# One activation table set in a fused DiT block, with layer-norm roots taken in pairs

## The chip, the cores and the metric

The kernel runs on one core of one Trainium2 chip. The metric is device time in microseconds (us); lower is better. Nearly every execution also leaves its span (first to last instruction, about 1.8 us shorter than the time) and its mean granted TensorE clock, where 1.0 is full speed. Ratios below are the mean time of one kernel's fast runs over that of the other's of the same rounds, so they are not quite the ratio of the medians quoted beside them.

## The reference, cut to what matters

```python
B, N, D = 2, 256, 1152          # F = 4 * D, two heads, bf16 inputs
mod = (silu(c) @ w_mod)         # shift_a, scale_a, gate_a, shift_m, scale_m, gate_m
h   = layernorm(x) * (1 + scale_a) + shift_a          # LN1
q, k, v = split(h @ wqkv)
a   = softmax(q k^T / sqrt(Dh)) @ v @ wo
x   = x + gate_a * a
h2  = layernorm(x) * (1 + scale_m) + shift_m          # LN2
out = x + gate_m * (gelu(h2 @ w_fc1) @ w_fc2)
```

## The kernel before

The 512 tokens are four tiles `t` of 128 rows: tiles 0 and 1 are batch 0, tiles 2 and 3 batch 1. While x and the first weights arrive, TensorE (PE) runs warm-up matmuls on zeros. LN1's statistics are split: VectorE (DVE) takes tiles 1 and 3, ScalarE (ACT) tiles 0 and 2. Each inverse root is a `pow` on GpSimd (Pool), one column at a time. Each normalized tile is transposed on PE, multiplied by 1 + scale ("modulate"), and fed to the K projection step by step. The order below is the program order on every engine.

```python
warm(8, pwarm)                    # fp32 matmuls on zeros
act_stats(0); act_stats(2)        # ACT: sums and sums of squares
...                               # DVE: bn_stats of tile 1
rsqrt1(1, True)                   # Pool: add eps, pow
act_mean(0)                       # Pool mean; DVE dm2; Pool dm2 += eps
act_var(0)                        # DVE
rsqrt1(0, False)                  # Pool: pow
norm1(1, 0, CUT)
stats_piece(3, 0)
norm1(0, 0, CUT)
stats_piece(3, 1); stats_piece(3, 2)
rsqrt1(3, True)
act_mean(2)
pt_a = transpose_x([0, 1], BT[0])         # PE, batch 0
add0 = scale_group(0, 1, acc_tile)        # 9 matmuls: scale chunk 0
add1 = scale_group(1, 2, acc_tile)        # 9 matmuls: scale chunk 1
add0()                                    # DVE: + 1
modulate(pt_a, 0, 0, 0, 0, "a")
act_var(2)
rsqrt1(2, False)
add1()
modulate(pt_a, 1, 1, 0, 0, "a")
norm1(3, 0, CUT); norm1(2, 0, CUT)
k_step(0, 0, N); k_step(1, 0, N, 0, 3)    # PE: K, batch 0
pt_c = transpose_x([0, 1], BT[1])         # PE, batch 1
...
# LN2, per tile: ACT Sqrt(var + eps), DVE reciprocal
```

## Time and profile before

| | before |
|---|---|
| median of the three first runs | 246.46 us (246.21 to 247.16) |
| the profiled execution | 245.73 us, span 244.0 us, clock 1.0 |
| PE busy | 237.0 us, 97% of the span |
| PE from 13.2 us on | 17.61 busy of 17.83 us up to 31 us, and no gap over 0.05 us in the chain after that |

From the profile's page: the span, PE's busy time, and the granted clock in 40 slices of 6.1 us (9 means 90% or more).

```profile
span 244.0 us, 3979 instructions
PE 237.0 (97%) x1688; PEld 145.0 (59%) x1698; DVE 91.2 (37%) x194; ACT 61.7 (25%) x117; POOL 30.1 (12%) x49
...
PEclk9999999999999999999999999999999999999999
```

PE is the limit almost everywhere, so time can only be won where PE waits: in the ramp at the start. The next view is the timeline of PE in that ramp (columns: start, duration, engine, line, operation, output and inputs, shape, count, and in brackets the idle time before it and what ended it).

```profile
9.20 0.38 PE L240 MATMUL pt<-ident,xn 128*128 128x128 bf16 x4 [0.40 <-ACT xn L191]
9.71 0.60 PE L230 MATMUL pm<-sT,w_scale_a 128*128 128x2 bf16 x18
10.89 0.71 PE L256 MATMUL pk<-big,w_k 128*128 128x256 bf16 x5 [0.57 <-ACT big L248]
11.97 0.27 PE L256 MATMUL pk<-big,w_k 128*128 128x256 bf16 x1 [0.37 <-DVE scale_a L234]
...
13.17 0.40 PE L240 MATMUL pt<-ident,xn 128*128 128x128 bf16 x4 [0.20 <-DVE xn L218]
```

L240 are the transposes (`pt`: first batch 0, then at 13.17 batch 1), L230 the modulation matmuls for the first two scale chunks, L256 the K projection. Why batch 1's transposes wait until 13.17 is told by the chain of waits (start, duration, what):

```profile
10.64 0.57 POOL rstd L215
11.21 0.26 POOL mv L198
11.47 0.19 POOL dm L204
...
11.93 0.74 POOL rstd L215
...
13.17 0.41 PE pt L240 x4
```

Two Pool powers (L215, 0.57 and 0.74 us), with a mean (L198) and an addition of eps (L204) on Pool and a variance on DVE between them, stand one after the other between batch 1's statistics and its transposes.

The ScalarE timeline has four table loads:

```profile
1.39 1.28 ACT L153 ACT_TABLE_LOAD   x1 [1.39 <-PEq L783]
54.54 1.28 ACT L524 ACT_TABLE_LOAD   x1
80.06 1.28 ACT L611 ACT_TABLE_LOAD   x1
107.20 1.28 ACT L697 ACT_TABLE_LOAD   x1 [1.36 <-issue]
```

Those at 54.54 and 80.06 us, ahead of softmax and LN2, are the two that the change removes.

### The profile page before, as it was taken

The page shows a single profiled execution, that of the slowest core. Times are in us where ns is not written, and L with a number is a line of the kernel's source. Part 1 is how long each engine was busy: PE and PEld are TensorE (multiplying, and loading weights), DVE is VectorE, ACT ScalarE, POOL GpSimd, SP SyncE. Part 2 cuts the span into 40 slices and gives each one's busy share as a digit, 9 for nine tenths or more (in the row PEclk, how much of TensorE's full clock was granted, in tenths as well). Part 3 has the DMA queues.
Part 4 walks back from the last instruction along what each step waited for, and adds up shares of the span by engine and source line. Part 5 has one row for each costly group of instructions (what it writes and reads, how often), then busy time and mean ns, then how long its engine had stood idle before and what let it go on. Part 6 is the DMA issues. An engine that isn't in the chain of part 4 may idle for free.

```text
span 244.0 us, 3979 instructions
## 1 busy us (share of the span) xinstructions
PE 237.0 (97%) x1688; PEld 145.0 (59%) x1698; DVE 91.2 (37%) x194; ACT 61.7 (25%) x117; POOL 30.1 (12%) x49
## 2 busy tenths in 40 slices
PE   8799999999999999999999999999999999999994
PEld 5575444456667556788854444444566666656574
DVE  3552542325515588932001999960010000000001
ACT  6623332235323321563432222332000000000000
POOL 2500000031000232300000000001112221111111
PEclk9999999999999999999999999999999999999999
DMA  6999999994779998248999999199630000000000
GB/s 209 323 317 319 380 370 390 391 392 167 172 235 396 391 377 133 47 81 294 394 388 392 350 327 318 33 336 326 194 108 16 20 16 16 20 16 16 24 28 16
DMA packets 48781, 53.29 MB, mean 218 GB/s; under 512 B 9587, under 2 KB 36475, under 8 KB 48763
## 3 DMA queue, kind: packets, MB, share of 16 engines
q1 hardware_dynamic: 41312, 50.14, 61.6%
q10 hardware_dynamic: 6939, 1.71, 4.6%
q0 software_dynamic: 512, 1.19, 1.6%
q8 instruction: 13, 0.21, 0.4%
q14 instruction: 5, 0.04, 0.1%
HBM read 50.14 MB, written 1.19 MB: 210 GB/s over the span
## 4 chain that ended last, share of the span: by engine, by line
PE 93%; DVE 2%; DMA 1%; POOL 1%; issue 1%; SPq 0%; POOLq 0%; DVEq 0%
PE pacc L744 29%; PE pacc L688 29%; PE pacc L634 7%; PE pacc L544 7%; PE pq L465 7%; PE pk L256 4%; PE pk L285 2%; PE pa L582 2%; PE ps_s L502 2%; PE pn L363 2%; DMA x_sb<-in_x_dram 1%; DVE stats L180 1%; PE pt L240 1%; POOL rstd L215 1%; PE pm L230 1%
## 5 line engine op out<-in xcount | busy, mean ns | idle before, releaser
L688 PE MATMUL pacc<-hT,w_f 128*128 128x256 bf16 (+1 forms) x427 | 70.3, 325 | 0.3
L744 PE MATMUL pacc<-w_f,gT 128*128 128x384 bf16 (+2 forms) x468 | 70.5, 314 | 0.0
L744 PEld LDWEIGHTS <-gT 128*128 128x128 bf16 x468 | 44.4, 98 | 26.2
L688 PEld LDWEIGHTS <-w_f 128*128 128x128 bf16 x432 | 42.2, 98 | 27.6
L750 DVE TENSOR_TENSOR tmp<-pacc,gate 128x384 f32<-128x384 f32 (+2 forms) x13 | 6.9, 527 | 65.6 <-PE pacc L744 55.0
L720 ACT ACTIVATE gT<-pacc 128x512 bf16<-128x512 f32 x24 | 14.3, 597 | 32.6 <-PE pacc L688 32.6
L416 DVE SCALAR_TENSOR_TENSOR part<-w_gate_m,s,part 128x1152 f32<-128x1152 bf16 x16 | 21.4, 1413 | 0.0
L634 PE MATMUL pacc<-w_o,big 128*128 128x384 bf16 x108 | 18.1, 326 | 0.0
L752 POOL TENSOR_TENSOR o_sb<-tmp,x 128x384 bf16<-128x384 f32 (+1 forms) x12 | 11.7, 972 | 51.8 <-DVE tmp L750 51.8
L465 PE MATMUL pq<-hT,w_q 128*128 128x512 bf16 x79 | 17.9, 379 | 0.1
L544 PE MATMUL pacc<-w_v,hT 128*128 128x384 bf16 x108 | 17.7, 326 | 0.0
L256 PE MATMUL pk<-big,w_k 128*128 128x256 bf16 (+1 forms) x70 | 13.4, 324 | 1.4 <-ACT big L248 0.8
L544 PEld LDWEIGHTS <-hT 128*128 128x128 bf16 x108 | 10.5, 98 | 7.1 <-issue 0.2
L634 PEld LDWEIGHTS <-big 128*128 128x128 bf16 x108 | 10.3, 98 | 7.3 <-issue 0.7
L465 PEld LDWEIGHTS <-w_q 128*128 128x128 bf16 x81 | 7.8, 98 | 9.4 <-issue 0.3
L640 POOL TENSOR_TENSOR x<-tmp,x_sb 128x384 f32<-128x384 f32 x8 | 7.3, 914 | 33.5 <-DVE tmp L639 33.5
L414 DVE TENSOR_SCALAR part<-w_gate_m,s 128x1152 f32<-128x1152 bf16 x2 | 1.5, 818 | 22.0 <-DMA w_gate_m<-in_w_mod_dram 22.0
L256 PEld LDWEIGHTS <-w_k 128*128 128x128 bf16 x72 | 6.7, 97 | 5.2 <-issue 1.8
L438 POOL DMA_DIRECT2D gates_dram<-nat_v x2 | 1.1, 536 | 67.5 <-DVE nat_v L436 67.5
L709 ACT ACTIVATE gT<-pacc 128x512 bf16<-128x512 f32 x12 | 6.5, 598 | 9.0 <-PE pacc L688 9.0
L162 PE MATMUL pwarm<-zeros 128*128 128x256 f32 x20 | 7.6, 549 | 1.2 <-DVE eps_t L93 1.2
L639 DVE TENSOR_TENSOR tmp<-pacc,gate 128x384 f32<-128x384 f32 x12 | 6.6, 551 | 3.7 <-PE pacc L634 3.7
(92 smaller groups left out, 163.2 us busy)
## 6 DMA issues: line engine op xcount, KB each, us to landing
w_f<-in_w_fc_dram SPq DMA_DIRECT2D x12, 864.0 KB, 14.8
w_f<-in_w_fc_dram SPq DMA_DIRECT2D x3, 1728.0 KB, 8.1
w_f<-in_w_fc_dram SPq DMA_DIRECT2D x2, 2592.0 KB, 18.2
w_gate_a<-in_w_mod_dram SPq DMA_DIRECT2D x3, 864.0 KB, 12.3
w_v<-in_wqkv_dram SPq DMA_DIRECT2D x3, 864.0 KB, 14.1
w_o<-in_wo_dram SPq DMA_DIRECT2D x3, 864.0 KB, 14.3
w_shift_m<-in_w_mod_dram SPq DMA_DIRECT2D x3, 864.0 KB, 6.5
w_scale_m<-in_w_mod_dram SPq DMA_DIRECT2D x3, 864.0 KB, 12.1
```

Of the source, the lines that this page charges most:

```text
L162: nc.tensor.matmul(dst[:, 0:T // 2], zeros32[:, 0:P], zeros32, start=True, stop=True)
L256: nc.tensor.matmul(pk[m][:, c0:c1], w_k[:, k, m * P:(m + 1) * P], hT0[:, k, c0:c1], start=(k == 0 and c0 == 0), stop=(k == KD - 1), skip_g ...
L416: nc.vector.scalar_tensor_tensor(part[:, b, :], wg[:, k, :], s32[:, k, b:b + 1], part[:, b, :], op0=ALU.mult, op1=ALU.add,)
L465: nc.tensor.matmul(pq[m][:], w_q[:, k, m * P:(m + 1) * P], hT[:, k, :], start=(k == 0), stop=(k == KD - 1), skip_group_check=True,)
L544: nc.tensor.matmul(pacc[:], hT[:, k, t * P:(t + 1) * P], w_v[:, k, pnl * PW:(pnl + 1) * PW], start=(k == 0), stop=(k == KD - 1),)
L634: nc.tensor.matmul(pacc[:], aT[:, k, t * P:(t + 1) * P], w_o[:, k, c0:c1], start=(k == 0), stop=(k == KD - 1),)
L640: (nc.gpsimd if pool_add else nc.vector).tensor_tensor(x1[:, t, c0:c1], tmp[:], x_sb[:, t, c0:c1], op=ALU.add)
L688: nc.tensor.matmul(dst, w_f1[m // KD][:, k, ml * P:(ml + 1) * P], hT[:, k, c0:c1], start=start, stop=(k == KD - 1), **kw,)
L720: nc.scalar.activation(gT[:, m, :], pacc[:], ACT.Gelu_apprx_tanh)
L744: nc.tensor.matmul(pacc[:], gT[:, kk, t * P:(t + 1) * P], w_f2[j][:, r, c0 - n * PW:c0 - n * PW + cw], start=(kk == 0), stop=(kk == KF - 1),)
L750: nc.vector.tensor_tensor(tmp[:], pacc[:], gate_m[:, b, c0:c0 + cw], op=ALU.mult)
L752: (nc.vector if last else nc.gpsimd).tensor_tensor(o_sb[:], tmp[:], x1[:, t, c0:c0 + cw], op=ALU.add)
```

## The change

The intent: Silu becomes c / (1 + exp(-c)), and LN2's inverse root becomes exp(-ln(var + eps) / 2), so Exp and Ln from one table set serve everything up to the Gelu. In LN1, batch 0's two roots become one two-column Pool pow, and batch 1's two roots an Ln and an Exp on ScalarE. The first two scale chunks share one PSUM tile (the buffer that the matmuls write to) and one addition, on ScalarE. The first modulate moves from ScalarE ("a") to VectorE ("d"), and the transposes go tile by tile, which the cut leaves out. Cut to its core:

```diff
-    nc.scalar.activation(early[:, 0:1], zeros[:, 0:1], ACT.Silu)
+    nc.scalar.add_instruction(mybir.InstLoadActFuncSet(act_func_set_id=6, ...))   # ln and exp
...
-    nc.scalar.activation(sT..., pc..., ACT.Silu)
+    nc.scalar.activation(sig[:], pc[:], ACT.Exp, scale=-1.0)
+    nc.vector.tensor_scalar_add(sig[:], sig[:], 1.0)
+    nc.vector.reciprocal(sig[:], sig[:])
+    nc.vector.tensor_tensor(sT..., pc..., sig..., op=ALU.mult)
...
+    def ln_exp_rsqrt(dst, var):
+        nc.scalar.activation(dst, var, ACT.Ln, bias=eps_t[:], scale=1.0)
+        nc.scalar.activation(dst, dst, ACT.Exp, scale=-0.5)
...                                           # the ramp
-    rsqrt1(1, True)
-    act_mean(0)
+    act_mean(0, True)
+    nc.gpsimd.tensor_scalar_add(mv1[:, 1, 1:2], mv1[:, 1, 1:2], LN_EPS)
     act_var(0)
-    rsqrt1(0, False)
-    norm1(1, 0, CUT)
+    var, rstd = pair(0)
+    nc.gpsimd.tensor_tensor(rstd, var, neg_half[:], op=ALU.pow)
     stats_piece(3, 0)
     norm1(0, 0, CUT)
+    norm1(1, 0, CUT)
     stats_piece(3, 1)
+    act_mean(2, False)
     stats_piece(3, 2)
-    rsqrt1(3, True)
-    act_mean(2)
+    act_var(2)
     pt_a = transpose_x([0, 1], BT[0])
-    add0 = scale_group(0, 1, acc_tile)
-    add1 = scale_group(1, 2, acc_tile)
-    add0()
-    modulate(pt_a, 0, 0, 0, 0, "a")
-    act_var(2)
-    rsqrt1(2, False)
-    add1()
+    add = scale_group(0, 2)
+    add()                                     # on ScalarE: Identity, bias 1
+    modulate(pt_a, 0, 0, 0, 0, "d")
+    var, rstd = pair(2)
+    ln_exp_rsqrt(rstd, var)
     modulate(pt_a, 1, 1, 0, 0, "a")
+    norm1(2, 0, CUT)
     norm1(3, 0, CUT)
-    norm1(2, 0, CUT)
...                                           # LN2
-        nc.scalar.activation(rstd[:], mv2[:, t, 1:2], ACT.Sqrt, bias=eps_t[:], scale=1.0)
+        ln_exp_rsqrt(rstd[:], mv2[:, t, 1:2])
-        nc.vector.reciprocal(rstd[:], rstd[:])
```

## The prediction

> What bounds the kernel now. TensorE: the page gives PE 237.0 of 244.0 us busy at full granted clock, and the chain of waits is 93% PE. From 13.17 us to the last output PE hardly waits (windows: 17.61 busy of 17.83 us up to 31 us, full after that). Before 9.20 us PE only runs warm-up matmuls. So time can be won only in the ramp from 9.2 to 13.2 us: there PE has 32 matmuls, some 1.9 us of work at the later pace, in 3.97 us. The waits list and the timeline name the stalls: 0.57 us before the first K matmul (behind the scale's add and ScalarE's 0.47 us modulate), 0.37 us on the second scale add's PSUM buffer, 0.24 us on the second modulate, and 0.2 us at 13.17 behind batch 1's norm. There the chain goes VectorE variance, Pool 0.22, 0.57, 0.27, 0.19 us, VectorE, Pool pow 0.73 us (to 12.67), norm, transposes.

> Removed. Two of four table loads, 1.28 us each in the timeline (at 54.5 us before softmax, 80.1 us before the Sqrt). Both are hidden: after the softmax load ScalarE still waits 2.64 us for VectorE, after the Sqrt load 6.93 us. Worth nothing. [...]

> Added. Silu's three VectorE instructions of 0.15 to 0.2 us run at 3.7 to 4.4 us, where VectorE idles until x lands at 4.46. Free.

> Moved. Batch 0: one Pool pow over two columns, my estimate 0.6 to 0.95 us, from 7.1 us. Normalizes start near 8.1 instead of 8.64 (now batch 0's second) and end near 8.9, transposes at 8.8 to 9.2. But the first scale weights land at 9.66 (PE weight load waited 0.30 us for them), so 18 modulation matmuls again run 9.71 to 10.31: this part wins nothing. Then ScalarE's add of one (0.28 us) and VectorE's 0.35 us modulate: first K matmul at about 11.05, 0.15 us later than now. ScalarE then does Ln and Exp (about 0.3 us each, to 11.2) and the second modulate (to 11.65), just in time for PE. Norms of batch 1 run 11.25 to 12.0 instead of 11.8 to 13.1, so its transposes start at about 12.1 to 12.2 instead of 13.17. From there PE is full as before: 1.0 us gained, and kept. Thin point: the third group of scale weights lands at about 15.9 and would be wanted at 16.3.

> LN2: Ln, Exp on ScalarE replace Sqrt and VectorE's reciprocal: rstd about 0.05 to 0.1 us later per tile (0.35 us for tile 2's modulates). PE has no wait there; the first FC1 matmul at 99.77 has about 0.35 us of slack. Zero.

> Predicted: 245.4 us, 244.5 to 246.4. Faster by over 2%: 0.01; within 2%: 0.98; slower by over 2%: 0.01.

> Signs that it's right: first batch 1 transpose near 12.1 us; first K matmul near 11.05; PE idle between 9.2 and 14 us down by 1 us; two table loads; the FC1 start and every later mark about 1 us earlier; no PE wait near 99 us.

> Wrong if: the two-column pow takes well over 1.4 us; the third variance comes late on VectorE and Ln waits; scale weights arrive late so PE stalls at 16 us; LN2's longer root delays the first FC1 matmul; a table load stays somewhere in the ramp.

The sum: 246.46 us less the ramp's 1.0 to 1.1 us (batch 1's transposes at 12.1 to 12.2 instead of 13.17) is 245.4 us; the table loads, the added VectorE instructions and LN2 count zero. The times of instructions that the kernel before doesn't have are estimates; its profile shows 0.57 to 0.73 us for a one-column pow on Pool, 0.29 us for a 128x1 Sqrt on ScalarE, 0.35 us for a VectorE modulate and 0.15 us for its addition of one.

## The result, and the profile after

The changed kernel takes 244.22 us (median of 4 runs, 244.12 to 244.6), before 246.49 us (4 runs), ratio 0.9907 (95% interval 0.9884 to 0.993). 2.3 us were gained where 1.06 was forecast, and 244.22 lies below the stated range. The gain between the two profiled spans is 1.6 us (244.0 to 242.4).

The page after:

```profile
span 242.4 us, 3980 instructions
PE 236.4 (98%) x1688; PEld 145.2 (60%) x1698; DVE 91.2 (38%) x192; ACT 59.8 (25%) x120; POOL 27.8 (11%) x45
...
PEclk9999999999999999999999999999999999999999
```

The table loads on ScalarE after. Two are left, as intended; LN1's Ln at 10.14 us and Exp at 10.46 us, softmax's exponentials and LN2's roots all run between them without a third:

```profile
1.39 1.28 ACT L153 ACT_TABLE_LOAD   x1 [1.39 <-PEq L799]
105.65 1.28 ACT L713 ACT_TABLE_LOAD   x1 [1.36 <-issue]
```

The timeline of PE in the ramp after (L258 transposes, L244 modulation, L274 K):

```profile
8.66 0.39 PE L258 MATMUL pt<-ident,xn 128*128 128x128 bf16 x4
9.28 0.60 PE L244 MATMUL pm<-sT,w_scale_a 128*128 128x2 bf16 x18 [0.23 <-DMA w_scale_a<-in_w_mod_dram]
10.68 1.14 PE L274 MATMUL pk<-big,w_k 128*128 128x256 bf16 x9 [0.80 <-DVE big L264]
11.66 0.39 PE L258 MATMUL pt<-ident,xn 128*128 128x128 bf16 x4
11.89 1.42 PE L274 MATMUL pk<-big,w_k 128*128 128x256 bf16 x9
```

The first K matmul starts at 10.68 instead of 10.89 us, batch 1's transposes at 11.66 instead of 13.17 us. After that PE is full again in both, and what follows is the same: from the first K matmul of batch 1 that waits for its modulate (14.01 and 12.49 us) to the first FC1 matmul it is 85.76 us in both (99.77 and 98.25), and from there to PE's end 141.03 us in both. The 1.52 us are won in the ramp and kept to the end. One sign of the prediction was missed: PE's idle time between 9.2 and 14 us fell from 1.63 to 0.99 us, by 0.64 us and not by 1 us. Part of the gain lies earlier, where the first transposes start at 8.66 instead of 9.20 us.

The chain of waits in the ramp after:

```profile
2.58 6.65 DMA w_scale_a<-in_w_mod_dram
...
9.28 0.62 PE pm L244 x18
...
9.98 0.27 ACT scale_a L250
...
10.68 1.14 PE pk L274 x9
```

Pool and the norms have left the chain. It now starts from the arrival of the first scale weights (`w_scale_a`), which landed at 9.23 us here; in the profile of before they landed at about 9.66 us.

That leaves two questions. The prediction had batch 1's transposes at 12.1 to 12.2 us: is the missing 0.45 us only the earlier landing, and is that luck or the change? And why is the gain by medians, 2.27 us, larger than the 1.6 us between the spans?

### The profile page after: what moved, and what is told of

Same layout as the page of the kernel before. It is cut to its first block, busy times and chain, and to the rows that moved or that the text cites. A ratio compares the mean times of both kernels' runs of the same rounds, so it can differ in the third digit from the quotient of the medians.

```text
span 242.4 us, 3980 instructions
## 1 busy us (share of the span) xinstructions
PE 236.4 (98%) x1688; PEld 145.2 (60%) x1698; DVE 91.2 (38%) x192; ACT 59.8 (25%) x120; POOL 27.8 (11%) x45
## 4 chain that ended last, share of the span: by engine, by line
PE 94%; DMA 3%; SPq 1%; DVE 1%; issue 0%; ACT 0%; DVEq 0%; ACTq 0%
PE pacc L760 29%; PE pacc L704 29%; PE pacc L650 7%; PE pacc L561 7%; PE pq L482 7%; PE pk L274 5%; DMA w_scale_a<-in_w_mod_dram 3%; PE pk L303 2%; PE pa L599 2%; PE ps_s L519 2%; PE pn L380 2%; PE pm L244 1%; PE pt L258 1%; SPq L86 1%; PE pg L462 0%
## 5 line engine op out<-in xcount | busy, mean ns | idle before, releaser
L768 POOL TENSOR_TENSOR o_sb<-tmp,x 128x384 bf16<-128x384 f32 (+1 forms) x12 | 11.6, 970 | 54.2 <-DVE tmp L766 54.2
L274 PE MATMUL pk<-big,w_k 128*128 128x256 bf16 (+1 forms) x70 | 13.1, 324 | 1.0 <-DVE big L264 0.8
L274 PEld LDWEIGHTS <-w_k 128*128 128x128 bf16 x72 | 6.7, 98 | 4.5 <-issue 1.1
```

Source lines behind the costliest of these rows:

```text
L274: nc.tensor.matmul(pk[m][:, c0:c1], w_k[:, k, m * P:(m + 1) * P], hT0[:, k, c0:c1], start=(k == 0 and c0 == 0), stop=(k == KD - 1), skip_g ...
L768: (nc.vector if last else nc.gpsimd).tensor_tensor(o_sb[:], tmp[:], x1[:, t, c0:c0 + cw], op=ALU.add)
```

## The experiments

Four runs went to each chip together, and each kernel was executed five or six times there, beside 11 executions of the kernel before. Every execution comes with a mean clock, and this is what turned out to matter. (It reads 1.0 also where nothing was recorded: the profiles of e4 and e9 hold no clock record. Their matmuls in the ramp took the times of the other full-clock profiles, 1.14 and 1.42 us for two groups of nine K matmuls, so these two were at full clock; for the other executions it can't be checked.) The table sums up all of them; "full clock" means a mean clock of 0.998 or more, "low clock" 0.993 or less; nothing lay between.

| kernel | executions | at full clock: mean time, mean span | at low clock: number, mean time |
|---|---|---|---|
| before (e1 and the three sets beside the experiments) | 39 | 20: 245.63, 243.83 | 19: 246.63 |
| changed (first result and e2) | 10 | 9: 244.26, 242.48 | 1: 246.30 |
| e3 tables only | 6 | 4: 245.61, 243.80 | 2: 246.51 |
| e4 changed, Sqrt in LN2 | 6 | 5: 244.74, 242.96 | 1: 246.06 |
| e5 before, gap filled | 6 | 5: 245.61, 243.84 | 1: 246.32 |
| e6 changed, gap filled | 6 | 6: 244.49, 242.72 | 0 |
| e7 changed, Pool pow for batch 1 | 6 | 4: 244.16, 242.40 | 2: 245.65 |
| e8 changed, split adds | 6 | 3: 244.21, 242.40 | 3: 245.60 |
| e9 before, pair for batch 1 | 6 | 2: 244.75, 242.95 | 4: 245.84 |
| e10 before, less warm-up | 6 | 0 | 6: 246.57 |
| e11 before, more warm-up | 6 | 6: 245.62, 243.82 | 0 |
| e12 changed, split adds, filled | 5 | 5: 243.88, 242.10 | 0 |

### e1 and e2: both kernels again, unchanged

> The kernel before, unchanged. Theory A (a third of the gain came from a first scale-weight transfer that happened to land at 9.23 us instead of 9.66): in this profile the first of the 18 modulation matmuls starts anywhere from 9.2 to 9.7 us, and the span moves along with it, 243.6 to 244.1. Rival B (the change itself makes that transfer land earlier): it starts at 9.6 to 9.8 again, as in the first profile of this kernel. Ratio 1.000 within 0.002 either way.

> The changed kernel, unchanged. Theory A: the first modulation matmul starts anywhere from 9.2 to 9.7 us, the first K matmul 1.4 us after it, batch 1's transposes 2.4 us after it; ratio near 0.995 when averaged over rounds. Rival B: it starts at 9.2 to 9.3 again and the ratio stays near 0.991.

Measured: e1 has ratio 1.0011 (0.9988 to 1.0034), e2 0.9945 (0.9913 to 0.9977). In e1's profile the first modulation matmul starts at 9.65 us, in e2's at 9.22 us. On these two alone the rival (B) looked no worse than theory A. What neither theory had foreseen was in the clocks. The kernel before has two groups of executions: 2 of e1's 6 at 0.998 to 0.999 with a span of 243.8 us, and 4 at 0.992 to 0.993 with 244.7 to 245.0 us. The 2.27 us of the first result thus compare mostly different clocks: all four times of before there (246.21 to 247.16) lie in the range of the low group (246.24 to 247.62 over all sets) or, in one case, 0.03 us under it, and none in that of the full one (245.59 to 245.85). Their clocks were not recorded, so this is read from the times. At full clock the change is worth 1.37 us in time and 1.35 us in span, about 0.6%.

### e3: the table set alone

```diff
 # before, plus only:
+ one Ln/Exp table set; Silu as Exp, add, reciprocal, multiply
+ LN2: rstd = exp(-ln(var + eps) / 2)
 # the LN1 ramp stays as it was
```

> Before, with only the one table set: Silu as Exp, add, reciprocal, multiply, and LN2 roots as exp of -ln/2; the two table loads go, the LN1 part stays as it was. Theory (loads are hidden): ratio 1.000 within 0.002, two table loads fewer in the timeline, ramp stalls as before (batch 1 transposes near 13.2 us). Rival (the loads, or the DMA traffic around them, cost something): ratio 0.995 or less.

Measured: ratio 0.9996 (0.9974 to 1.0017); at full clock 243.80 us, as before. Two loads are left in the timeline (1.37 and 108.06 us). The removed loads were worth nothing, as predicted. (Batch 1's transposes came at 13.54 us in the profile, not near 13.2: it was a low-clock execution.)

This profile shows what a low clock is. The windows view: each line gives a stretch in us from the start, its length, PE's busy time in it with the count of matmuls, the granted clock, and the DMA share and rate. The stretches are those of the clock record.

```profile
4.97:8.39 3.42, 2.97 (x14) 1.00 0.97 292
8.39:11.80 3.41, 1.34 (x27) 1.00 1.14 327
11.80:15.21 3.41, 2.94 (x16) 0.50 1.15 321
15.21:18.62 3.41, 3.41 (x58) 1.00 1.16 313
```

### e4: the Sqrt load put back

```diff
 # changed kernel, LN2:
-        ln_exp_rsqrt(rstd[:], mv2[:, t, 1:2])
+        nc.scalar.activation(rstd[:], mv2[:, t, 1:2], ACT.Sqrt, bias=eps_t[:], scale=1.0)
 ...
+        nc.vector.reciprocal(rstd[:], rstd[:])
```

> The changed kernel, with LN2's root taken as Sqrt and reciprocal again, so a Sqrt table load comes back before LN2. Theory (hidden): same time as the changed kernel within 0.2%. Rival (the load removed there was worth up to 1.3 us): 0.3 to 0.5% slower than the changed kernel.

Measured: ratio to before 0.9957 (0.9932 to 0.9981), against 0.9945 for the changed kernel; a load is back at 78.91 us. By full-clock means e4 is 0.48 us (0.2%) slower than the changed kernel: at the very edge of what the theory allowed, and less than the rival asked for. The PE timeline of its ramp:

```profile
9.64 0.60 PE L244 MATMUL pm<-sT,w_scale_a 128*128 128x2 bf16 x18 [0.43 <-DMA w_scale_a<-in_w_mod_dram]
11.05 1.14 PE L274 MATMUL pk<-big,w_k 128*128 128x256 bf16 x9 [0.81 <-DVE big L264]
12.03 0.39 PE L258 MATMUL pt<-ident,xn 128*128 128x128 bf16 x4
```

The profile does not support the rival either: PE's list of waits holds nothing after the ramp, and the ramp, whose code is that of the changed kernel, explains the profiled span. Its first scale weights landed late: modulation starts at 9.64 us, the first K matmul at 11.05, batch 1's transposes at 12.03, and the span is 242.8. Two further executions had spans of 243.3 and 243.4 us, and without their traces it is open whether their weights came later still or their clock was low unrecorded. That the load costs nothing rests on e3 and on this list of waits, not on e4's time.

### e5 and e6: fill PE's gap

```diff
     add1 = scale_group(1, 2, acc_tile)       # e6: after add = scale_group(0, 2)
+    warm(2, pwarm)
```

> Before, plus two warm-up matmuls (0.27 us each) on PE right after the first 18 modulation matmuls, where PE waits 0.55 us for the first modulate. Theory C (about half the executions of the kernel before lose 0.9 us because the granted clock halves for some 3 us after the thinly filled ramp): with the gap filled, executions with a clock of 0.991 to 0.993 become rare, at most 1 in 6, and all sit near a span of 243.8; mean ratio 0.998. Rival D (the low clock comes at random, whatever the ramp does): still 2 to 4 of 6 executions at 0.992 and 244.8.

> The changed kernel, plus two warm-up matmuls right after the first 18 modulation matmuls, where PE waits 0.80 us. Theory C: no execution at a clock near 0.992, spans 242.2 to 242.9 in all. Rival D: about 1 in 6 slow, as without them.

Measured: one low-clock execution of 6 in e5 and none in e6, while 3 of 11 of the kernel before were low on this chip. This fits theory C but does not settle it. Two forecasts were missed: e5's ratio was 0.9996 (0.9978 to 1.0015) rather than 0.998, and one of e6's spans was 243.4 us, beyond the 242.9 expected (the others 242.3 to 242.7; e6's ratio 0.9945, 0.9927 to 0.9962). (Two warm-up matmuls took 1.11 us rather than the 0.54 written down: each is two instructions. In e6 that just filled the gap: the first K matmul came 1.41 us after the first modulation matmul, as without them.)

e5's profile answers the question about landing for the kernel before. Its modulation starts at 9.23 us, as early as in the changed kernel, so early weights are not the change's doing. They brought it almost nothing: batch 1's transposes began at 12.97 us against 13.05 in e1, where modulation began at 9.65, with a span of 243.8 in both. Before, the norm chain of batch 1 sets the pace; in the changed kernel it is the landing, as long as that comes late enough (e7).

### e7: batch 1's roots on Pool

```diff
-    var, rstd = pair(2)
-    ln_exp_rsqrt(rstd, var)
+    # placed after act_var(2); act_mean(2, True), eps added to tile 3 on Pool
+    nc.gpsimd.tensor_tensor(rstd, var, neg_half[:], op=ALU.pow)
```

> The changed kernel with batch 1's roots as one two-column Pool pow instead of ScalarE's Ln and Exp. Theory E (what helped batch 1 is the earlier statistics and the pairing, not the engine): the pow is done near 10.6 us, as the Exp was (10.66), and time is equal to the changed kernel within 0.1%. Rival F (the scalar engine's root is what wins): batch 1's transposes move from 11.6 to 12.1 or later, span 0.4 us longer or more.

Measured: ratio 0.9951 (0.9925 to 0.9977) with two of six at low clock; at full clock 242.40 us against 242.48 for the changed kernel. The pow ended at 10.87 us, the Exp of the changed kernel at 10.66. In time Pool did as well as ScalarE, as theory E had it. But the profiles compared differ in their weights: the PE timeline of this run has the earliest of all:

```profile
8.69 0.59 PE L244 MATMUL pm<-sT,w_scale_a 128*128 128x2 bf16 x18
...
11.37 0.61 PE L258 MATMUL pt<-ident,xn 128*128 128x128 bf16 x4
```

Modulation started at 8.69 us, 0.59 us earlier than in the profile after, and the span is the same 242.4: with early weights, the norm chain is the limit again (DVE waited 0.85 us for the Pool pow), and batch 1's transposes follow the first K matmul by 1.27 us where it is 0.98 us in the profile after. With ScalarE's root and weights nearly as early, e12's Exp ended at 10.31 us and its transposes again followed by 0.98 us. So for early weights it is not shown that Pool is as good; these two profiles speak for ScalarE. The same transfer, issued at 2.57 (e4) to 2.58 us (before, after), landed anywhere from 8.63 us at the latest (e7, where its weights were loaded into PE then without a wait) to 9.67 us (before): with the ramp code of before or near it by 9.18 us (e5, without a wait too) to 9.67, with the changed one by 8.63 (e7) to 9.60 (e4). The two ranges overlap, so the early landing of the first profile after was a draw and not the change's doing.

### e8: two adds on VectorE again

```diff
-    add = scale_group(0, 2)
-    add()                              # ScalarE
+    add0 = scale_group(0, 1, acc_tile)
+    add1 = scale_group(1, 2, acc_tile)
+    add0()                             # VectorE
     modulate(pt_a, 0, 0, 0, 0, "d")
     var, rstd = pair(2)
     ln_exp_rsqrt(rstd, var)
+    add1()
```

> The changed kernel with the first two scale groups again as two PSUM tiles in the accumulator pool and two VectorE adds. Theory G (the wait for the first scale weights and what follows it sets the pace): the first add follows 9 matmuls instead of 18, the first K matmul comes 1.0 to 1.1 us after the first modulation matmul instead of 1.4, and the span shrinks by 0.2 to 0.4 us. Rival H (merging the groups was part of the gain): PE waits for a PSUM buffer or for the second modulate by 0.3 us or more, and the span is equal or longer.

Measured: ratio 0.9962 (0.9931 to 0.9992), because 3 of 6 executions were at low clock. The profiled one was at full clock:

```profile
9.56 0.60 PE L244 MATMUL pm<-sT,w_scale_a 128*128 128x2 bf16 x18 [0.55 <-DMA w_scale_a<-in_w_mod_dram]
10.58 1.14 PE L273 MATMUL pk<-big,w_k 128*128 128x256 bf16 x9 [0.41 <-DVE big L263]
```

The weights landed as late as in e4 and e6 (9.56 us), yet the first K matmul follows 1.02 us later. In the profiles of the changed kernel, e4, e6 and e2 it is 1.40 to 1.41 us each time. The span is 242.3 where e4 and e6 had 242.8 and 242.7. So, with late weights, theory G holds: the merged addition on ScalarE cost time. The traces tell its two parts from each other. The add starts 0.42 us after the first modulation matmul instead of 0.70 us, because it waits for 9 matmuls and not 18, and on VectorE it takes 0.16 us instead of 0.26. Over all full-clock executions little is left of it: e8's mean span is 242.40 us (three executions) against 242.48, not the 0.2 to 0.4 us less that was forecast. The idle gap that it leaves is shorter, but the clock was low more often; six executions do not say whether that is chance.

### e9: the pair alone, in the kernel before

```diff
     stats_piece(3, 1)
-    stats_piece(3, 2)
-    rsqrt1(3, True)
     act_mean(2)
+    stats_piece(3, 2)
+    nc.gpsimd.tensor_scalar_add(mv1[:, 3, 1:2], mv1[:, 3, 1:2], LN_EPS)
+    act_var(2)
+    nc.gpsimd.tensor_tensor(rstd1[:, 2:4], <var of tiles 2, 3>, neg_half[:], op=ALU.pow)
 ...
-    act_var(2)
-    rsqrt1(2, False)
```

> Before, with one thing of the change in LN1 alone: batch 1's two roots in one two-column Pool pow, its mean terms started one statistics piece earlier. Silu, Sqrt, four table loads, batch 0's two pows, the split scale groups stay. Theory (the serial Pool chain of batch 1 was what PE waited for): pow done near 11.4 instead of 12.7 us, batch 1's transposes at 12.2 to 12.3 instead of 13.1, span 243.0 at full clock, that is 0.8 us of the 1.35 us. Rival (the gain needs the merged scale group or the ScalarE roots): span 243.6 or more.

Measured: ratio 0.9961 (0.9932 to 0.9989), with 4 of 6 at low clock. At full clock the spans are 242.9 and 243.0 us, as expected.

```profile
10.84 1.14 PE L256 MATMUL pk<-big,w_k 128*128 128x256 bf16 x9 [0.68 <-ACT big L248]
12.13 0.40 PE L240 MATMUL pt<-ident,xn 128*128 128x128 bf16 x4
```

Batch 1's transposes start at 12.13 us instead of 13.1. So 0.88 us of the 1.35 us come from this one edit (by the mean of two full-clock executions), with Silu, Sqrt, four table loads and everything of batch 0 as they were. The edit pairs the two roots and starts mean and variance earlier; how much each of these is worth was not separated. It also takes PE's wait for the second scale addition away, since that addition no longer queues behind batch 1's variance on VectorE.

### e10 and e11: theory C, pushed both ways

```diff
-    warm(8, pwarm)
+    warm(5, pwarm)        # e10
+    warm(10, pwarm)       # e11, and warm(2, pwarm) after the first modulation matmuls
```

> Before, with 5 instead of 8 warm-up matmuls ahead of the first transposes, so PE is idle some 1.5 us longer there. Theory C (the clock halves when one window of 3.41 us holds too little PE work): 4 or more of 6 executions carry a half-clock window (mean clock 0.993 or less), median 0.5 us or more above before. Rival D (low clock at random): 2 or 3 of 6, as before.

> Before, with 10 instead of 8 warm-up matmuls ahead of the first transposes and two more after the first modulation matmuls. Theory C: no execution with a half-clock window; full-clock span 243.8 to 244.2. Rival D: 2 or 3 of 6 still have one.

Measured: with less warm-up all 6 executions had a low clock, with more none, and on the same chip 7 of 11 of the kernel before. This bears theory C out; low clocks at random would not follow the dose. Median of e11 245.61 us, ratio 0.9966 (0.9942 to 0.999), although nothing in the ramp runs earlier: its full-clock span is 243.8 to 243.9. e10's median was only 0.09 us above before, not 0.5, because most of before's own executions were low there; against before's full-clock mean (245.63) e10's median of 246.69 is 1.06 us longer. The windows of e10, then of e11:

```profile
5.86:9.27 3.41, 1.29 (x9) 1.00 1.05 310
9.27:12.68 3.41, 2.52 (x30) 0.50 1.14 322
12.68:16.10 3.42, 3.42 (x37) 0.50 1.15 318
```

```profile
6.67:10.08 3.41, 3.41 (x36) 1.00 1.12 333
10.08:13.50 3.42, 2.84 (x25) 1.00 1.15 318
```

In e10 a window with 1.29 us of PE work was followed by two at half clock (four of its six executions have a mean clock of 0.986, which fits two such windows in 245 us; the other two 0.992 and 0.993, which fit one). In e11 the two windows across the ramp held 3.41 and 2.84 us, and the clock stayed up. Where the line lies is not shown; the least that kept the full clock in our profiles was 2.04 us (before, 10.33 to 13.75 us), the most at full clock that lost it 1.34 us.

### e12: split adds and fillers together

```diff
 # e8, plus two half-width warm-up matmuls
+    def fill(dst):
+        nc.tensor.matmul(dst[:, 0:P], zeros32[:, 0:P], zeros32[:, 0:P], start=True, stop=True)
 ...
+    fill(pwarm)
     add0 = scale_group(0, 1, acc_tile)
     add1 = scale_group(1, 2, acc_tile)
+    fill(pwarm)
```

> The changed kernel with split VectorE adds (as e8) and two half-width warm-up matmuls (0.27 us each), one before and one after the first modulation matmuls. Theories C and G: spans 242.1 to 242.5 in nearly all executions, at most 1 of 6 with a half-clock window, so the mean is 0.2 us or more under the changed kernel's, ratio to before 0.993. Rival: half-clock windows as often as in e8 (3 of 6), mean not better than the changed kernel.

Measured: correct, median 243.82 us over 5 executions (243.76 to 244.07), ratio 0.9896 (0.987 to 0.9922), all at full clock, spans 242.0 to 242.3.

```profile
8.97 0.60 PE L247 MATMUL pm<-sT,w_scale_a 128*128 128x2 bf16 x18
9.44 0.47 PE L174 MATMUL pwarm<-zeros 128*128 128x128 f32 x2
10.24 1.14 PE L276 MATMUL pk<-big,w_k 128*128 128x256 bf16 x9 [0.34 <-DVE big L266]
11.22 0.39 PE L260 MATMUL pt<-ident,xn 128*128 128x128 bf16 x4
```

The second filler (L174 at 9.44, 0.47 us; the first is at 8.63, 0.44 us; 0.27 was expected of each) sits in PE's wait for the first modulate. This is 0.38 us under the changed kernel's full-clock mean and 0.59 us under its mean over all executions (244.47). That comparison is across chips; before's full-clock mean was 245.61 to 245.66 us on all three. What made e12 0.33 us faster than e8 at full clock (243.88 against 244.21) is not shown: the fillers do not shorten e12's ramp, where the first K matmul comes 1.27 us after the first modulation matmul instead of 1.02 (VectorE came to the first add only at 9.65 us, after batch 1's statistics), and in the one profile the weights landed early, by 8.97 us, when their modulation began.

## Why the prediction was right or wrong

Right: PE bounds the kernel, and only the ramp could win time. The two table loads were worth nothing (e3). Silu's VectorE instructions were free: statistics began at 4.39 us, not later than the 4.48 before. The pair pow took 0.72 us, inside 0.6 to 0.95, where a single column took 0.57 to 0.73 us before (0.57 both times that it followed Pool's own addition of eps). In LN2, from the start of the root to the start of the normalize took 0.87 us instead of 0.83 (Ln 0.29 and Exp 0.20 us on ScalarE, before Sqrt 0.29 us and VectorE's reciprocal 0.16), and PE did not wait there. Batch 1's norm chain was the thing to shorten, and the gain stayed to the end.

Wrong, first: the baseline. The prediction subtracted a gain read from a full-clock profile from 246.46 us, a median of low-clock executions. It called the clock "full" from that one profile and did not ask why the profiled execution (245.73 us) was faster than all the timed ones. The first result then compared about 246.5 us, low, with 244.2 us, full: some 0.9 us of its 2.27 us. Over all executions the means are 246.12 and 244.47, a gain of 1.65 us: 1.37 us from the ramp, and about 0.3 us because 1 of 10 was at low clock instead of 19 of 39. Against 245.73 us the predicted gain would have given 244.7 us.

Wrong, second: "the first scale weights land at 9.66 (...): this part wins nothing". The durations after the landing were right: 0.74 us were allowed from the end of modulation to the first K matmul, and 0.79 us measured. But 9.66 us was one draw. Before, an earlier landing hardly helped (e5), so the draw was invisible; after the change the ramp hangs on it. In the profiles where it came late (e4, e6: 9.64 and 9.58 us) batch 1's transposes began at 12.03 and 11.97 us, close to the predicted 12.1, and the spans, 242.8 and 242.7 us, give a gain of 1.0 to 1.1 us against 243.83, the predicted one. Where it came earlier (9.28, 9.22) it was 1.4 us. The 20 full-clock executions with this ramp (changed, e4 and e6 together, if the other edits of e4 and e6 cost nothing) have a mean span of 242.67 us, a gain of 1.16 us (1.28 us without the three of 243.3 to 243.4 us, whose clock may have been low unrecorded), so part of the 1.35 us looks like luck of the draw. The predicted chain in the ramp was right in size for late weights. Of the 1.21 us between the forecast 1.06 and the measured 2.27, 0.90 us come from the baseline's clock and 0.31 us from the ramp, where the earlier weights explain them as far as the profiles go.

Open: whether the changed kernel itself has fewer low-clock executions. 1 of 10 (2 of 16 with e4, which has the same ramp) against 19 of 39 says so, but e7 and e8, whose ramps differ little, had 5 of 12. Shown is only that PE work in the ramp decides it (e10, e11). Also open is what spreads the landing of the weights: it was seen to vary, but no run set it. And the 0.47 us of the 1.35 us beyond e9's edit were not divided among batch 0's pair, the moved modulate and the rest.

## What to carry to other kernels

Before sizing a change of half a per cent, look at the clock and span of every execution rather than the median: a baseline that mixes two clock states can hide or swell the gain (here 1.37 us at full clock read as 2.27). Look for the serial chain that PE waits on; here one paired root on a side engine, started earlier, was worth two thirds of a change whose headline, the table loads, was worth nothing. When a chain has been shortened, the next limit takes over with its own spread, and a few dummy matmuls in a start-up gap can be worth a good part of the rescheduling: e11 is 0.50 us under before's mean over all executions, where the change gives 1.37 us at full clock.
